# RWKV-7 recurrence and gated MoE on one core: the running product of w by a product tree over DRAM, in place of transposes, scan and transposes back

## The chip, the cores and the metric

One core of one Trainium2 chip. The time is device time in microseconds (us) of one execution, from the start of the program on the core to its end. The profile comes from one more execution, whose own time is given beside its span, the stretch from the first to the last instruction.

The engines are named as in the profile: PE is TensorE (PEld its weight loads), DVE is VectorE, ACT is ScalarE, POOL is GpSimd, SP is SyncE, which here does nothing but issue DMAs.

## The reference

B, H, S, D = 4, 8, 768, 40: four batches, eight heads, 768 tokens, 40 elements of a head. All inputs are float32.

```python
state = zeros(B, H, D, D)
for t in range(S):
    y[t]  = einsum('bhd,bhde->bhe', r[t], state)
    Sa    = einsum('bhde,bhe->bhd', state, a[t])
    state = state * w[t][:, :, None, :] - einsum('bhd,bhe->bhde', Sa, b[t])
    state = state + einsum('bhd,bhe->bhde', v[t], k[t])
x = y as (B*S, H*D)                       # 3072 x 320
h = x @ w_in                              # 320 x 2048
out = (h * cos(h)) @ w_out                # 2048 x 320
```

Only `w` and `a` matter for what follows. `w` decays each column of the state, so inside a chunk of tokens everything can be written with the running product W(t) = w(0) w(1) ... w(t), taken elementwise within the chunk: `a~` is a(t) times W(t-1), and k and b are divided by W(t).

## The kernel before

**Chunks.** The 768 tokens are cut into 24 chunks of C = 32. A natural tile (`nat[n, c]`, n one of w, a, b, k, v, r) has 128 partitions, batch times token, and in each partition 8 heads of 40 elements, padded to 64 for w, a and b (`DP`). Each such tile is loaded by `load` (L146): four DMAs, one for each batch, of 40 KB each. From chunk 4 on the tiles of w, a and b are double buffers, so a load waits until every reader of the tile two chunks earlier is done.

**W of a chunk.** `p1_w` (L331) does two chunks at a time. `turned` (L298) puts w by four PE transposes into PSUM as `wT`: partitions are (one of two heads, d), and the free axis is (pair of heads, batch, token), so tokens now lie in a row. ACT copies the first token of each row into `w1` (L336), DVE sets those places of `wT` to zero (L337), and a DVE scan over 512 elements (L340) computes state = state * w + w1. That is the running product, restarted at each row, and it is written to `wb`. POOL takes the last token's product as `wc` (L342), by which the state is decayed at the end of a chunk.

**What needs W in which layout.** `p1_a(c)` (one chunk at a time) brings W back by four PE transposes of `wb` into PSUM, `wn` (L353), because b and k need it as natural tiles. POOL then writes 1.0 into each row's first place of `wb` (L357), by which the same tile read one place earlier (`wx`) is W(t-1). PE transposes a into `aps`; DVE takes the reciprocal `rw` of `wn` (L361) and multiplies `aps` by `wx` to `aT` (L363); POOL multiplies b by `rw` to `bn` (L366). From chunk 4 on `wn` and `aps` share one PSUM tile. `p1_b` transposes `bn` of two chunks and ACT copies it (`bT`, L375); `p1_n` multiplies `bT` and `aT` for every batch and head into `nps`, and ACT copies the result into `nt` (L393).

**The inverse.** The unit triangular systems of four chunks are solved at once on DVE by `inverse`: a stream transpose `u` (L406), 31 steps of two instructions (L414, L418) and a stream transpose back, `rt` (L422). It begins when `nt` of four chunks is there.

**The recurrence of a chunk.** `main(c)` has five parts, which follow each other strictly: `ch_t` transposes the state `qz` (`sT`, L504; ACT copies `s`, L508), `ch_q` multiplies it by r (`qps`), `ch_x` builds the right side (`x0ps`, from `aT`, `qz`, `ag` and `vvm`), `ch_s` multiplies by `rt` (`sps`), and `ch_z` updates state and output (`dps`; `qz` on DVE and POOL L602/L603; `yt` L609/L614, the last times `wx`). Zeros that start a PSUM group in `ch_z` come from a matmul on the zero tile `idle`. Beside them `p2` prepares k, v, r of the next chunk: `p2_v` (`vT`, `rT`), `p2_k` (`kT`), `p2_g` (`gram`, `ag` L487, `vvm` L492).

**To the MoE.** `tokens(c)` writes `yt` to DRAM as `xd` (two DMAs, L623), and one step later `back` reads it as `xT` (three DMAs, L633/L635). Two chunks make one group of 256 tokens. A group and a quarter of d_ff are worked in pieces: `first_a` and `first_b` (`ph`, through the helper L101), the cosine by turns (ACT L676, DVE L678, ACT L682 and L683), the product `gT` (DVE L686), and two `second` (`po`, also L101), each of which goes out to DRAM after the last quarter.

**Weights of the MoE.** They come as 8-byte words, which `rounded` (L192) turns into float32: `fetch` (SP), `taken` (DVE and ACT), `mantissa` (DVE and ACT), `product` (DVE L229, POOL L232). These steps are spread over the first three chunks of the main loop.

**Order.** Nothing is scheduled automatically: every engine executes its instructions in the order in which the program issues them, and waits at each until its inputs and its output buffer are free. For each chunk a list `segs` holds the parts in that order; `M` is the place of an MoE piece. `step` issues one part, then the work that `later(n, work)` put n steps off (mostly DMA issues), then a few steps of the inverse and of the weights (`fill`). SP's queue is therefore also in program order: a DMA that waits holds those behind it.

```python
elif c == 2:
    segs, fill = [t, v, q, k, M, x, M, g, M, s, M, z, M, M], (0, 2)
```

`busy` and `shifted(N_PAD[c])` issue small PE matmuls whose results nobody reads; `shifted` stands at the head of chunks 2 and 19. PSUM has three pools with two buffers each: `ps_a` (two banks, `at(...)`: `wT`, `wn`, `bT`, `nps`, `sT` and so on), `ps_h` (`ph`) and `ps_o` (`po`).

Of the kernel before, what the change touches and what calls it, by code (L numbers as in the profile page):

```python
# [20 lines left out]
def kernel(  # L21
# [124 lines left out]
    def load(c, names, via=nc.sync):  # L146
        for n in names:
            for i in range(B):
                via.dma_start(
                    nat[n, c][blk[i], :, :D],  # L150
                    src[n][i, :, c * C : (c + 1) * C, :].rearrange("h t d -> t h d"),
                )

    for c in range(2):
        load(c, "w")
        load(c, "a", nc.scalar)
    for n, c in (("b", 0), ("b", 1), ("w", 2), ("w", 3), ("b", 2), ("b", 3)):
        load(c, n)
    load(0, "kvr")

# [14 lines left out]
    w1 = kept("w1", [P, 4 * B, C], 2, 0.0, on=nc.vector)  # L175
# [9 lines left out]
    idle = const.tile([P, 512], BF16, tag="idle", name="idle")  # L185
# [144 lines left out]
    def p1_w(c):  # L330
        ps = at("wT")  # L331
        for i in range(2):
            turned(ps[:, i], nat["w", c + i])

        for i in range(2):
            nc.scalar.copy(w1[i][:, :, 0:1], b4(ps[:, i])[:, :, 0:1])  # L336
        nc.vector.memset(ps[:, :, ::C], 0.0)  # L337
        for i in range(2):
            wb = ring.tile([P, 4 * P + 1], F32, tag="wb", name="wb")
            nc.vector.tensor_tensor_scan(wb[:, 1:], ps[:, i], flat(w1[i]), 0.0, ALU.mult, ALU.add)  # L340
            wc = ring.tile([P, 4 * B], F32, tag="wc", name="wc")
            nc.gpsimd.tensor_copy(wc, wb[:, C::C])  # L342
            G["wb", c + i], G["wc", c + i] = wb, wc

    def p1_a(c):
        if c < 4:
            wn = ps_h.tile([P, 512], F32, tag="h", name="wn")
            aps = ps_o.tile([P, 512], F32, tag="o", name="aps")
        else:
            ps = at("wn")  # L350
            wn, aps = ps[:, 0], ps[:, 1]
        for j in range(4):
            nc.tensor.transpose(  # L353
                wn[:, j * P : (j + 1) * P], G["wb", c][:, j * P + 1 : (j + 1) * P + 1], ident
            )

        nc.gpsimd.memset(G["wb", c][:, : 4 * P : C], 1.0)  # L357
        G["wx", c] = b4(G["wb", c][:, : 4 * P])
        turned(aps, nat["a", c])
        rw = ring.tile([P, H, D], F32, tag="rw", name="rw")  # L360
        nc.vector.reciprocal(rw, unpad(wn.rearrange("p (h d) -> p h d", h=H)))  # L361
        aT = ring.tile([P, 4, P], F32, tag="aT", name="aT")
        nc.vector.tensor_tensor(  # L363
            aT.rearrange("p j (b t) -> p (j b) t", b=B), b4(aps), G["wx", c], ALU.mult
        )
        nc.gpsimd.tensor_tensor(unpad(bn_b[c % 7]), unpad(nat["b", c]), rw, ALU.mult)  # L366
        G["rw", c], G["aT", c] = rw, aT
# [207 lines left out]
    def ch_z(c):  # L575
# [3 lines left out]
        for bb in range(B):  # L579
            for e in range(2):  # L580
                mm(
                    ps[bb // 2][full[e], bb % 2, : 4 * N72], idle[blk[bb], :DP],
                    idle[blk[bb], : 4 * N72], True,
                )
# [147 lines left out]
    def p1(c):  # L732


        def first_w():
            p1_w(c)
            if c == 4:
                for i in range(2):
                    later(1, lambda i=i: load(6 + i, "w"))

        def an_a(i):
            p1_a(c + i)
            if c == 4:
                later(1, lambda: load(6 + i, "ab"))
            elif i and c >= 2 and c + 3 < NCH:
                for m in range(6):
                    later(
                        9 + m // 3 if c == 2 else 2 + m, lambda m=m: load(c + 2 + m % 2, "wab"[m // 2])
                    )

        return [first_w, lambda: an_a(0), lambda: an_a(1), lambda: p1_b(c), lambda: p1_n(c)]
# [17 lines left out]
    with tc.manual_schedule():  # L769
# [24 lines left out]
        def busy(n, after=False):  # L794


            ps = ps_h.tile([P, 512], F32, tag="h", name="busy")
            if after:
                nc.vector.memset(tick, 1.0)
                nc.tensor.matmul(  # L800
                    ps[:1, :], lhsT=tick, rhs=idle, start=True, stop=True, skip_group_check=True
                )
            for _ in range(n):
                mm(ps, idle[:, :P], idle, True)
# [10 lines left out]
        for seg in (*first[:3], *other[:3], *first[3:], *other[3:]):  # L815
            step(seg)
# [5 lines left out]
        for n, seg in ((12, v), (0, k), (0, g), (6, main(0)[2]), (6, None), (4, v1), (0, k1), (0, g1)):  # L822
            for _ in range(n):
                inv_steps.pop(0)()
            if seg:
                step(seg)
            else:
                for m in range(3):
                    w_work[m][0]()
                p2_in(1)  # L830
                p2_kn(1)
        while inv_steps:
            inv_steps.pop(0)()
            if 2 < len(inv_steps) < 9:
                busy(1, True)
# [16 lines left out]
        N_PAD = {2: 56, 19: 48}  # L852
        M = object()
        for c in range(NCH):
# [8 lines left out]
            elif c == 2:  # L863
                segs, fill = [t, v, q, k, M, x, M, g, M, s, M, z, M, M], (0, 2)
            elif c == 3:
                pw4, pa4, pa5, pb4, pn4 = p1(4)
                pw, pa, pa1, pb, pn = p1(6)
                segs = [
                    t, pw4, M, q, pa4, M, x, pa5, M, s, pw, M, pb4, pa, M, pn4, pa1, M, z, M, pb, v,
                    pn, k, M, g,  # L870
                ]
                fill = (2, 3)
            elif c == 4:
                pw, pa, pa1, *p8 = p1(8)
                segs = [t, v, M, q, M, k, x, M, g, M, s, M, z, M, pw, M, pa, pa1, M]
                fill = (2, 0)
            elif c == 5:
                pw, pa, pa1 = p1(10)[:3]
                pb, pn = p8
                segs = [t, M, pb, q, M, pn, v, M, x, k, M, s, pw, M, g, M, z, M, pa, pa1, M]  # L880
            elif c % 4 == 0 and q0 < NCH:
                pb, pn = p1(q0)[3:]
                segs = [t, v, M, q, M, k, x, M, g, M, s, pb, M, z, M, pn, M, M]
            elif c % 4 == 1 and q0 < NCH:
                pw, pa, pa1 = p1(q0 + 2)[:3]
                segs = [t, M, pw, q, M, x, k, M, s, v, M, z, M, pa, M, g, M, pa1, M]
            elif c % 4 == 2 and q0 < NCH:
                pb, pn = p1(q0 + 2)[3:]
                segs = [t, M, pb, q, M, pn, v, M, x, M, s, k, M, g, M, z, M, M]
            elif c % 4 == 3 and q0 + 4 < NCH:  # L890
                fill = (2 if c == 7 else 1, 0)
                pw, pa, pa1 = p1(q0 + 4)[:3]
                segs = [t, M, pw, q, M, x, k, M, s, v, M, z, M, pa, M, g, M, pa1, M]
            else:
                segs = [t, v, M, q, M, x, k, M, g, M, s, M, M, z, M, M]
# [8 lines left out]
            if c in (2, 19):  # L904
                shifted(N_PAD[c])
# [58 lines left out]
```

## Time and profile before

| | |
|---|---|
| time, median of 3 runs | 847.02 us (846.65 to 847.22) |
| profiled execution: its own time | 844.89 us |
| profiled execution: span | 842.9 us, mean granted PE clock 0.952 |
| chain that ended last, by engine | PE 65%, DVE 23%, ACT 5%, issue 3%, DMA 2% |
| DMA | 49.10 MB, mean 58 GB/s |
| MoE matmuls `po`, `ph` (with its tail) | 226.4, 189.4 and 54.5 us of PE |
| inverse, L414 and L418 | 70.8 and 68.5 us of DVE |

The page is of one profiled execution. Part 1 gives each engine's busy time; part 2 cuts the span into 40 slices of 21 us and gives the busy share of each in tenths; part 4 follows the last instruction back to what released it; part 5 lists groups of instructions as "line engine operation output<-inputs shape xcount | busy, mean ns of one | idle time of the engine just before them, and what ended most of it". The timeline adds to each instruction its start in the span and its duration, and in square brackets a wait ahead of it with what ended it.

### The profile page before, as it was taken

The numbers are of one execution on the slowest core, as the hardware profiler recorded it, in microseconds if no ns is written. First come the engines' busy times: TensorE is split into PE (matmuls) and PEld (weight loads), VectorE is DVE, ScalarE is ACT, GpSimd is POOL, SyncE is SP. The second block draws the span as 40 slices with busy tenths as digits, with TensorE's granted clock in tenths as the row PEclk, the third lists the DMA queues.
The fourth block names the chain that finished last, engine by engine and source line by source line (L and its number), as shares of the span: only waits on it lengthen the run. The fifth ranks groups of instructions, "written<-read, shape, count | busy, mean of one in ns | idle before, by whom it ended". The sixth has DMA issues, their size and how long they took to land.

```text
span 842.9 us, 37607 instructions
## 1 busy us (share of the span) xinstructions
PE 750.5 (89%) x16830; PEld 575.3 (68%) x16830; DVE 511.0 (61%) x1076; ACT 377.1 (45%) x707; POOL 197.1 (23%) x343
## 2 busy tenths in 40 slices
PE   3547877995998979999998999998999999999997
PEld 3424556774676757778776777776777877777775
DVE  7688878778534696335797345796354774323331
ACT  1216676353153433545435436435445444454343
POOL 4405634230303203203221221230221222011000
PEclk9758698998898999999999999999999999999999
DMA  7456453431133212313224214214211212101000
GB/s 97 101 92 183 128 152 87 65 67 31 40 53 60 57 35 50 67 36 68 49 41 76 51 27 73 52 39 73 56 25 36 46 26 48 36 20 35 19 16 16
DMA packets 181856, 49.10 MB, mean 58 GB/s; under 512 B 156992, under 2 KB 178496, under 8 KB 181696
## 3 DMA queue, kind: packets, MB, share of 16 engines
q1 hardware_dynamic: 179264, 46.05, 26.6%
q8 instruction: 132, 2.16, 1.1%
q10 hardware_dynamic: 2176, 0.33, 0.3%
q0 software_dynamic: 256, 0.33, 0.2%
q14 instruction: 28, 0.23, 0.1%
HBM read 38.80 MB, written 7.86 MB: 55 GB/s over the span
## 4 chain that ended last, share of the span: by engine, by line
PE 65%; DVE 23%; ACT 5%; issue 3%; DMA 2%; SPq 1%; POOL 0%; ACTq 0%; DVEq 0%; POOLq 0%
PE ph L101 22%; PE po L101 19%; DVE inv_tmp L414 5%; DVE inv L418 5%; PE dps L101 3%; PE x0ps L101 3%; PE gram L101 2%; PE vT L298 2%; PE sps L101 2%; PE nps L101 2%; DVE turns L678 1%; DVE wb L340 1%; DVE rw L361 1%; PE qps L101 1%; PE bT L298 1%
## 5 line engine op out<-in xcount | busy, mean ns | idle before, releaser
L101 PE MATMUL po<-w_out_sb,gT 128*128 128x320 f32 x768 | 226.4, 442 | 0.0
L101 PE MATMUL ph<-xT,w_in_sb 128*128 128x256 f32 x768 | 189.4, 392 | 4.1 <-DVE gT L686 3.3
L101 PEld LDWEIGHTS po<-w_out_sb,gT 128*128 128x128 f32 x768 | 140.8, 191 | 54.1 <-issue 3.0
L101 PEld LDWEIGHTS ph<-xT,w_in_sb 128*128 128x128 f32 x768 | 143.1, 195 | 33.0 <-issue 12.9
L676 ACT ACTIVATE turns<-ph,rnd 128x512 f32<-128x512 f32 x96 | 63.8, 686 | 160.8 <-PE ph L101 160.2
L678 DVE SCALAR_TENSOR_TENSOR turns<-turns,ph 128x512 f32<-128x512 f32 x96 | 63.7, 684 | 110.0 <-ACT turns L676 109.8
L603 POOL TENSOR_TENSOR qz<-qz,wc 128x160 f32<-128x160 f32 x92 | 42.6, 482 | 254.5 <-DVE qz L602 254.0
L686 DVE TENSOR_TENSOR gT<-ph,turns 128x512 f32<-128x512 f32 x96 | 65.8, 686 | 36.8 <-ACT turns L683 36.8
L414 DVE TENSOR_TENSOR inv_tmp<-u,inv 128x31 f32<-128x31 f32 (+15 forms) x186 | 70.8, 381 | 4.5
L418 DVE TENSOR_TENSOR inv<-inv,inv_tmp 128x31 f32<-128x31 f32 (+15 forms) x186 | 68.5, 369 | 6.4
L683 ACT ACTIVATE turns<-turns,half_pi 128x512 f32<-128x512 f32 x96 | 69.3, 722 | 3.1
L682 ACT ACTIVATE turns<-turns 128x512 f32<-128x512 f32 x96 | 60.2, 627 | 21.5 <-DVE turns L678 21.5
L361 DVE RECIPROCAL rw<-wn 128x320 f32<-128x320 f32 x24 | 51.6, 2150 | 8.0 <-PE wn L298 7.7
L101 PE MATMUL ph<-xT,w_in_tail 64*128 64x256 f32 x384 | 54.5, 402 | 0.0
L602 DVE TENSOR_TENSOR qz<-dps,qz 128x160 f32<-128x160 f32 x92 | 28.9, 315 | 34.2 <-PE dps L101 34.1
L508 ACT COPY s<-sT 128x512 f32<-128x512 f32 x46 | 24.5, 585 | 51.9 <-PE sT L504 51.9
L101 PEld LDWEIGHTS ph<-xT,w_in_tail 64*128 64x128 f32 x384 | 33.0, 186 | 10.4 <-issue 6.8
L614 POOL TENSOR_TENSOR yt<-yt,wb 128x512 f32<-128x512 f32 x24 | 31.2, 1302 | 22.3 <-DVE yt L609 22.3
L436 POOL COPY vp<-nat_v 128x320 f32<-128x320 f32 x25 | 11.9, 475 | 99.4 <-DMA nat_v<-in_v_dram 69.3
L101 PE MATMUL sps<-x,rt 32*32 32x72 f32 x1536 | 22.3, 239 | 13.1 <-DVE rt L422 10.9
L101 PEld LDWEIGHTS sps<-x,rt 32*32 32x32 f32 x1536 | 17.8, 109 | 23.2 <-issue 16.5
L492 ACT COPY vvm<-gram 128x256 f32<-128x256 f32 x24 | 8.8, 367 | 51.7 <-DVE ag L487 51.4
(117 smaller groups left out, 1070.8 us busy)
## 6 DMA issues: line engine op xcount, KB each, us to landing
words<-in_moe_w_in_dram SPq DMA_DIRECT2D x8, 512.0 KB
nat_k<-in_k_dram SPq DMA_DIRECT2D x96, 40.0 KB
nat_v<-in_v_dram SPq DMA_DIRECT2D x96, 40.0 KB
nat_r<-in_r_dram SPq DMA_DIRECT2D x96, 40.0 KB
xd<-yt SPq DMA_DIRECT2D x48, 80.0 KB
out_dram<-ot SPq DMA_DIRECT2D x24, 160.0 KB
nat_w<-in_w_dram SPq DMA_DIRECT2D x88, 40.0 KB
nat_b<-in_b_dram SPq DMA_DIRECT2D x88, 40.0 KB
```

What stands on the lines that cost most here:

```text
L101: nc.tensor.matmul(o, lhsT=lhsT, rhs=rhs, start=start, stop=stop, skip_group_check=True)
L361: nc.vector.reciprocal(rw, unpad(wn.rearrange("p (h d) -> p h d", h=H)))
L414: nc.vector.tensor_tensor(tmp, u[:, j : j + 1, :j].to_broadcast([P, C - j, j]), x[:, j:, j : j + 1].to_broadcast([P, C - j, j]), ALU.mult,)
L418: nc.vector.tensor_tensor(x[:, j:, :j], x[:, j:, :j], tmp, ALU.subtract)
L602: nc.vector.tensor_tensor(z, pick(dp, 0, (2 * N72 + C, 2), (N72, 2), (1, D)), z, ALU.add)
L603: nc.gpsimd.tensor_tensor(z, z, wc.rearrange("p (f m b) -> p f m b", f=2, m=2)[:, :, :, bb] .unsqueeze(3).to_broadcast([P, 2, 2, D]), ALU. ...
L614: nc.gpsimd.tensor_tensor(yt.rearrange("p j b t -> p (j b) t"), yt.rearrange("p j b t -> p (j b) t"), wx, ALU.mult)
L676: nc.scalar.activation(n, u, ACTF.Identity, bias=rnd, scale=1.0)
L678: nc.vector.scalar_tensor_tensor(n, n, -ROUND, u, ALU.add, ALU.subtract)
L682: nc.scalar.activation(n, n, ACTF.Abs)
L683: nc.scalar.activation(n, n, ACTF.Sin, bias=half_pi, scale=-2.0 * math.pi)
L686: nc.vector.tensor_tensor(gT[:, 2 * e : 2 * e + 2].rearrange("p f t -> p (f t)"), us[e], ns[e], ALU.mult)
```

## The change

W is no longer scanned in the transposed layout. `w` of four chunks is fetched as one tile `ws` with (batch, head, chunk) in the 128 partitions and 32 tokens of 40 elements in each, 655 KB (`ws_fetch`). Nine DVE multiplications in place turn it into running products over the tokens, five up a tree and four down (`ws_scan`). The result is written to a DRAM tile `wd`, and the loads of w read from `wd` instead of from the input: `nat["w", c]` now holds W itself.

So `p1_w` has no scan: ACT copies the transposed W to `wb`, and POOL takes `wc` and writes the 1.0 there. The reciprocal (`over_w`) reads the natural tile directly, and the transposes back (`wn`) are gone with `w1` and its resets. `p1_a` handles both chunks of a pair in one part (one PSUM tile `aps` from chunk 4 on), with the second chunk's reciprocal after both `aT`; before chunk 4 each chunk's reciprocal stands ahead of its `aT`. `over_w` of a pair's first chunk stands in `p1_w` from chunk 4 on.

The trees stand on DVE: the first at the start; the second in chunk 2 as a part of its own after `ch_t`; the third in chunk 3 after `ch_x`; the fourth late in chunk 4; the others late in chunks 8 and 12. The fetch for the next tree follows three steps after a tree. In chunk 2 the loads of w for chunks 4 and 5 follow one step after the tree; those of a and b for these chunks come as before, a step earlier in number.

The padding of chunk 2 (56 small matmuls) becomes 128 at the start, ahead of the end of the first inverse; that of chunk 19 goes from 48 to 79. The tile `idle` is 128 wide instead of 512 and is read with a stride of 0 where 512 columns are wanted.

```diff
+                at_c = wd[c // 4][i, :, c % 4] if n == "w" else src[n][i, :, c * C : (c + 1) * C, :]
+                via.dma_start(nat[n, c][blk[i], :, :D], at_c.rearrange("h t d -> t h d"))
...
+    def ws_fetch(q, via=nc.sync):
+        n = 4 * C * D
+        via.dma_start(
+            ws.rearrange("p t d -> p (t d)"),
+            bass.AP(w.tensor, w.offset + q * n, [[S * D, B * H], [C * D, 4], [1, C * D]]),
+        )
+
+    def ws_scan(q, via=nc.sync):
+        n = 1
+        while n < C:
+            to = ws[:, 2 * n - 1 :: 2 * n]
+            nc.vector.tensor_tensor(to, to, ws[:, n - 1 :: 2 * n], ALU.mult)
+            n *= 2
+        n = C // 4
+        while n:
+            to = ws[:, 3 * n - 1 :: 2 * n]
+            nc.vector.tensor_tensor(to, to, ws[:, 2 * n - 1 : C - 1 : 2 * n], ALU.mult)
+            n //= 2
+        wd[q] = dram.tile([B, H, 4, C, D], F32, tag="wd", name="wd")
+        via.dma_start(wd[q].rearrange("b h c t d -> (b h c) (t d)"), ws.rearrange("p t d -> p (t d)"))
+
+    ws_fetch(0)
     for c in range(2):
+        load(c, "a", nc.scalar)
+    ws_scan(0, nc.scalar)
+    for c in range(2):
+        load(c, "b")
+    for c in range(4):
         load(c, "w")
-        load(c, "a", nc.scalar)
-    for n, c in (("b", 0), ("b", 1), ("w", 2), ("w", 3), ("b", 2), ("b", 3)):
-        load(c, n)
+    for c in range(2, 4):
+        load(c, "b")
     load(0, "kvr")
+    ws_fetch(1)
...
-        for i in range(2):
-            nc.scalar.copy(w1[i][:, :, 0:1], b4(ps[:, i])[:, :, 0:1])
-        nc.vector.memset(ps[:, :, ::C], 0.0)
         for i in range(2):
             wb = ring.tile([P, 4 * P + 1], F32, tag="wb", name="wb")
-            nc.vector.tensor_tensor_scan(wb[:, 1:], ps[:, i], flat(w1[i]), 0.0, ALU.mult, ALU.add)
+            nc.scalar.copy(wb[:, 1:], ps[:, i])
             wc = ring.tile([P, 4 * B], F32, tag="wc", name="wc")
             nc.gpsimd.tensor_copy(wc, wb[:, C::C])
+            nc.gpsimd.memset(wb[:, : 4 * P : C], 1.0)
+            G["wx", c + i], G["wc", c + i] = b4(wb[:, : 4 * P]), wc
+        if c >= 4:
+            over_w(c)
+
+    def over_w(c):
+        rw = ring.tile([P, H, D], F32, tag="rw", name="rw")
+        nc.vector.reciprocal(rw, unpad(nat["w", c]))
+        nc.gpsimd.tensor_tensor(unpad(bn_b[c % 7]), unpad(nat["b", c]), rw, ALU.mult)
+        G["rw", c] = rw

     def p1_a(c):
-        for j in range(4):
-            nc.tensor.transpose(
-                wn[:, j * P : (j + 1) * P], G["wb", c][:, j * P + 1 : (j + 1) * P + 1], ident
-            )
...
+        if c >= 4:
+            ps = at("aps")
+        for i in range(2):
+            if c < 4:
+                aps = (ps_h, ps_o)[i].tile([P, 512], F32, tag="ho"[i], name="aps")
+            else:
+                aps = ps[:, i]
+            turned(aps, nat["a", c + i])
+            if c < 4:
+                over_w(c + i)
+            aT = ring.tile([P, 4, P], F32, tag="aT", name="aT")
+            nc.vector.tensor_tensor(
+                aT.rearrange("p j (b t) -> p (j b) t", b=B), b4(aps), G["wx", c + i], ALU.mult
+            )
+            G["aT", c + i] = aT
+        if c >= 4:
+            over_w(c + 1)
...
+    def scanned(q):
+        ws_scan(q)
+        if q == 1:
+            for i in range(2):
+                later(1, lambda i=i: load(4 + i, "w"))
+        if q + 1 < NCH // 4:
+            later(3, lambda: ws_fetch(q + 1))
...
-                segs, fill = [t, v, q, k, M, x, M, g, M, s, M, z, M, M], (0, 2)
+                segs, fill = [t, lambda: scanned(1), v, q, k, M, x, M, g, M, s, M, z, M, M], (0, 2)
...
                 segs = [
-                    t, pw4, M, q, pa4, M, x, pa5, M, s, pw, M, pb4, pa, M, pn4, pa1, M, z, M, pb, v,
-                    pn, k, M, g,
+                    t, pw4, M, q, pa4, M, x, lambda: scanned(2), M, s, pw, M, pb4, pa, M, pn4, M, z, M,
+                    pb, v, pn, k, M, g,
                 ]
...
-                segs = [t, v, M, q, M, k, x, M, g, M, s, M, z, M, pw, M, pa, pa1, M]
+                segs = [t, v, M, q, M, k, x, M, g, M, s, M, z, M, pw, M, pa, lambda: scanned(3), M]
...
-                segs = [t, M, pw, q, M, x, k, M, s, v, M, z, M, pa, M, g, M, pa1, M]
+                segs = [t, M, pw, q, M, x, k, M, s, v, M, z, M, pa, M, g, M, M]
...
-        N_PAD = {2: 56, 19: 48}
+        N_PAD = {0: 128, 19: 79}
+        shifted(N_PAD[0])
```

## The prediction, made before the changed kernel ran

> **What bounds the kernel now.** First the page's busy shares and slices: they say which stage has which limit.
>
> ```profile
> PE 750.5 (89%) x16830; PEld 575.3 (68%) x16830; DVE 511.0 (61%) x1076; ACT 377.1 (45%) x707; POOL 197.1 (23%) x343
> PE   3547877995998979999998999998999999999997
> DVE  7688878778534696335797345796354774323331
> PEclk9758698998898999999999999999999999999999
> ```
>
> A slice is 21 us. From slice 16 TensorE (PE) is full, so work taken from it there is time. In the first seven VectorE (DVE) is full and PE is not; there a chain sets the time. Then the waits of PE (columns: total, times, longest) and the group rows name what the change touches:
>
> ```profile
> PE sps L101 <- DVE rt L422: 10.9, 2, 9.2
> PE wn L353 <- DVE wb L340: 8.3, 3, 3.9
> PE vT L298 <- DVE aT L363: 8.0, 3, 3.8
> L340 DVE TENSOR_TENSOR_SCAN wb<-wT,w 128x512 f32<-128x512 f32 x24 | 28.1, 1212 | 0.4
> L361 DVE RECIPROCAL rw<-wn 128x320 f32<-128x320 f32 x24 | 51.6, 2150 | 8.0 <-PE wn L298 7.7
> ```
>
> Scan and reciprocal cost DVE 80 us, and PE waits for their results some 16 us. Last, the timeline where the new transfers will stand:
>
> ```profile
> 31.73 1.25 DVE L406 STREAM_TRANSPOSE u<-nt 128x1024 f32<-128x1024 f32 x1 [5.11 <-ACT nt L393]
> ...
> 101.24 1.75 DVE L229 TENSOR_TENSOR w_out_sb<-mant,expo 128x512 f32<-128x512 f32 x1
> 102.47 0.72 SPq L623 DMA_DIRECT2D xd<-yt  x2
> 105.83 0.93 DVE L229 TENSOR_TENSOR w_in_sb<-mant,expo 128x512 f32<-128x512 f32 x1
> 105.90 0.38 SPq L633 DMA_DIRECT2D xT<-xd  x1
> 109.67 1.89 PE L101 MATMUL ph<-xT,w_in_sb 128*128 128x256 f32 x8
> ...
> 453.83 0.63 PE L298 MATMUL vT<-ident,vp 128*128 128x128 f32 x4 [3.77 <-DVE aT L363]
> ```
>
> The first inverse starts at 31.73; the first MoE matmul starts at 109.67, 2 us after SyncE's queue issued xT.
>
> [...]31, 256 and 512 elements take 0.19, 0.42 and 0.69 us, that is 0.16 us + 1.04 ns an element. [...]L229 took 1.75 us beside GpSimd work, 0.69 alone. [...]xT took 2.0 us (chain, 260.26 to 262.26); the busiest 4 us of this execution (40 to 44, by stretches) moved 324 GB/s. [...]after PE's 9.24 us wait the clock reads 0.50 from 208 to 216, and eight po take 4.63 us instead of 2.3.
>
> **The parts.** A product tree over four chunks is nine multiplies on 640, 320, 160, 80, 40, 40, 120, 280 and 600 elements: 9 x 0.16 + 2280 x 1.04 ns = 3.8, with 25 ns between dependent ones **4.0 us**. Six trees (24 us) replace 24 scans (28.1) and their resets (1.0), so DVE gains little in sum; the place matters.
>
> *Start.* Now w goes from DRAM to the transposes. In the changed program it is fetched as 128 rows (655 KB, issued 0.81; landing about 6.0 beside a and b, as the first two w chunks needed until 5.5 and 9.5), multiplied (4.0, with seven memsets of 0.21 in between: end 11.5), written (issue 0.45, [...]655 KB at 324 GB/s 2.0: lands 16.0) and read back by 16 DMAs on SP at 0.49 each (eight took 3.9): chunk 1 is issued by 20 and lands at 22. Then, with cold transposes (0.87 for four), copies of 0.59 and 2.15 + 0.63 for reciprocal and aT: wT 23.1, wb 24.2, aT(0) 24.8, rw(1) 27.0, bn(1) 27.9, bT 28.8 and copies 29.9, nps 30.8, aps(2, 3) 32.5, with aT(2) in that at 32.3, rw(3) 34.5, bn(3) 35.4, bT 36.3, copies 37.3, nps 38.2, nt 39.3. The inverse starts at 39.3 instead of 31.7: **+7.6** (6.0 to 9.5). The 128 pads (24.6 ns each by the 56 that took 1.5 us at 100 us) are 3 to 6 us in a PE wait of over 6 us for DVE: 0.
>
> *Chunk 2.* The second tree stands on DVE behind the L229 of 105.83, so at 106.76. GpSimd's L232 holds it 1.3 us: end 112.1. On SP the write of wd stands ahead of xd and waits for the tree; behind xd stand two weight loads, then eight loads of w(4), w(5), which wait for the write, then xT. So: write issued 112.5, landed 116.8; eight loads 3.9: 120.7; xT issued 121.0, landed 123.0 to 124.4 when the write moves at half that rate. PE was ready at 108.2 (the 56 pads gone): it waits about 15 us[...]. Against 109.67: 14.7 + 1.7 = **+16.4** (12 to 19.5). Removing the pads saves nothing here. Nothing behind absorbs it: x0ps, the x copy and the recurrence stand behind that ph on PE. The eight w loads of 40.95 (6.2 us of SP) go, but there SP is not late.
>
> *Chunk 3.* PE's 3.9 us wait for the scan and its half clock go: aps needs only a. ACT's qz now waits for a mant behind rw(4): x0ps about 145.6 instead of 149.9, -4.3. But nat_w(7) now waits for rw(5) on DVE, 16 loads and another write stand behind it on SP, so xT of chunk 3 comes at 180.3 where PE would want it at 178.5; 1.5 of that reaches the inverse. **-2.8** (0 to -4.5). The 9.2 us wait for rt stays: u and rt move together.
>
> *Chunks 4 to 23* (20 chunks). Four wn transposes are 0.44 us of full PE a chunk. Chunk 4: two chunks' 0.88, the wait for aT at sT 1.8, and wn behind the scan 0.7; the third tree costs 0.7 back at turns: **-2.7**. Chunk 5: 0, its pieces end in the chain xd, xT, ph (254 to 262). Chunk 7: DVE is full (9.4 to 9.6 of 10 us), so its two scans and reset, 2.4, count; plus 0.88 and a 0.4 wait of vT: **-3.7** (-1.5 to -5). Chunks 9, 13, 17: 3 x 0.88 = **-2.6**. Chunks 11, 15: vT waits 3.77 each because the second wn tile is held until the second reciprocal and aT; now both aT come first. 2 x (3.77 + 0.88) = **-9.3**, and the half clock after the one at 575 **-1.4** (0.79 in 574 to 582). The wb copies (24 x 0.59 - 3.1 = 11 us) lie on ACT at 45%: 0. Trees 4, 5 lie in DVE at 40 to 75%: **+0.5** (0 to 3). The trees' writes block SP until they are done, but xd and xT of those chunks stand ahead of them, and k, v, r behind are needed a chunk later. Pads at chunk 19: 79 for 48, 31 x 24.6 ns: **+0.8**.
>
> *Costed at nothing.* Fetches and writes add 12 x 655 KB = 7.9 MB to 49.1, where the 16 DMA engines are 10 to 40% busy; only their place in the queue counts. The reciprocal reads SBUF instead of PSUM; no row shows that. The nearest pair does: the 256-element product takes 0.42 us from SBUF (inv_tmp) and from PSUM (ag). So I take 2.15 and allow 0.1 either way, 2.4 us over 24 at most, most of it beside a full PE. GpSimd keeps its operations: wc and the reset of wb to one move from behind scan and wn to behind the copy, earlier; bn follows rw as before. The narrow zero tile is read with stride 0 for the same columns, so PE does the same.
>
> Sum: 7.6 + 16.4 - 2.8 - 2.7 - 3.7 - 2.6 - 9.3 - 1.4 + 0.5 + 0.8 = **+2.8 us**. The profiled execution is 844.9 us (span 842.9 and 2.0 around it), so 847.7 there; the median of the runs is 847.0, so **849.8**.
>
> **Rivals.** *B, faster: the xT wait is short.* It decides at chunk 2: if that costs under about 12 us, that is if ph starts before 120, the rest gains. With no sharing (tree ends 110.7), the write at the page's rate (111.1 + 3.5 = 114.6) and loads at the shortest SP issue seen (0.31, 2.5 us), xT lands at 119.4: cost 11.4; with a start of +6.0 the sum is -3.8: 843. For it: issues of 0.31 exist; against: eight w loads in a row took 3.9 to 6.2 in every place. *C, slower: SP becomes the bound through chunk 4.* At 0.6 us an issue (eight a took 5.0) chunk 2 costs 19, and some 45 issues between rw(5) and xT of chunk 3 add 5, so chunk 3 gives +3 instead of -2.8: about 859. Against: the SP rows between 140 and 180 are nearer 0.49. *D: the change does not do what it says*, xT not behind the loads: the program order of SP shows it behind, so little is left.
>
> **Numbers.** A (the sum) 0.57, B 0.23, C 0.18, D 0.02. A measurement of this kernel can tell about 0.2%, 1.7 us, from no change. A's 2.8 with an error of some 4 gives slower 0.43, same 0.12, faster 0.02; B faster 0.21, same 0.02; C slower 0.18; D faster 0.01, slower 0.01. So faster 0.24, same 0.14, slower 0.62. A's own range is 844 to 855; taking in B and most of C: 840 to 860. Signs are mixed, because +24 and -22 nearly cancel and each is known to a few us.
>
> **What would show it.** u (the first stream transpose) at 37 to 41; the first ph at 120 to 129 with a wait of 10 us or more on DMA xT, and SP's nat_w loads just ahead; nine ws multiplies adding to 4 us; no PE waits on wb, and none of vT on aT at chunks 11 and 15; from the first sps of chunk 4 to the end about 18 us less. It is wrong if the first ph follows the tree within 8 us, if a tree takes over 6 us, or if the late stage gains under 12.

## The result, and the profile after

The changed kernel takes **874.89 us** (median of 4 runs, 874.65 to 875.50) against 846.84 (846.19 to 847.22): a ratio of 1.0333, 95% interval 1.0315 to 1.0351. It is 28 us slower. Forecast were 849.8 us, and 840 to 860 as the range.

The page of the profiled execution of the changed kernel (span 873.0 us, granted clock 0.930): busy time, two rows of slices, and the row of the reciprocal.

```profile
PE 755.9 (87%) x16840; PEld 576.6 (66%) x16840; DVE 506.2 (58%) x1092; ACT 384.6 (44%) x706; POOL 197.8 (23%) x343
...
PE   1547748788689897999998999989999999999997
...
DVE  4688856776863479455389454697444775323322
...
PEclk9757768899898998999999999999999999999999
...
L377 DVE RECIPROCAL rw<-nat_w 128x320 f32<-128x320 f32 x22 | 47.2, 2143 | 7.9 <-DMA nat_w<-wd 7.9
```

DVE is busy 5 us less than before, ACT 8 us more (11 were costed). PE lost the 16.3 us of transposes back and is still busy 5 us more, so its other work took longer. Beyond that the page says only that PE's gaps got larger (755.9 of 873.0, against 750.5 of 842.9). PE's waits of the changed kernel name them (total, times, longest):

```profile
PE wT L328 <- DMA nat_w<-wd: 18.7, 2, 18.4
PE aps L328 <- DVE aT L393: 16.0, 10, 3.5
PE sps L101 <- DVE rt L453: 10.0, 2, 8.5
PE ph L101 <- DMA xT<-xd: 9.3, 3, 4.1
PE kT L328 <- issue: 7.3, 2, 6.5
...
PE aps L328 <- ACT wb L366: 2.3, 1, 2.3
```

The waits of `wn` for `wb` (8.3 us) and of `vT` for `aT` (8.0) are gone. In their place stand two that the kernel before did not have and the prediction did not name: `aps` for `aT`, ten times, once for each pair of chunks from 4 on, and `aps` for ACT's copy `wb`, once.

To see where the 30 us of the two spans (873.0 - 842.9) lie, take the start of the first `sm` on DVE of a chunk (part `ch_s` of the recurrence; L568 before, L599 after) and subtract the two executions. The differences of these offsets are what each stage cost:

| stage, by the first `sm` of chunk | forecast | changed | with the transposes first (e1) |
|---|---|---|---|
| start to 1 | +7.6 | +5.9 | +6.5 |
| 1 to 2 | +16.4 | +14.3 | +13.2 |
| 2 to 4 | -2.8 | +6.1 | +7.4 |
| 4 to 6 | -2.7 | -0.1 | -1.9 |
| 6 to 18 | -16.5 | -0.3 | -13.5 |
| 18 to the end | +0.8 | +4.3 | +3.1 |
| sum | +2.8 | +30.2 | +14.7 |

The two large losses, start and chunk 2, came in about the size that was forecast. **The gains that should have paid for them did not come**: 16 us in the late chunks and 9 in chunks 2 to 4.

The timeline of PE in the changed kernel at one of the ten waits (start, duration, in brackets the wait):

```profile
403.27 1.99 PE L101 MATMUL ph<-xT,w_in_sb 128*128 128x256 f32 x8
405.11 0.60 PE L328 MATMUL aps<-ident,nat_a 128*128 128x128 f32 x4
406.56 0.66 PE L328 MATMUL aps<-ident,nat_a 128*128 128x128 f32 x4 [0.85 <-DVE aT L393]
407.05 1.89 PE L101 MATMUL ph<-xT,w_in_sb 128*128 128x256 f32 x8
```

The four transposes of the first chunk end, PE stops until `aT` of that chunk has been computed on DVE, then come the four of the second chunk. Behind them wait MoE matmuls that need neither. Here DVE takes `aT` at once and 0.85 us is lost; at 469 and 591, where DVE is late, 3.5 us.

Chunk 2 in the changed kernel, all engines, shortened:

```profile
117.58 0.33 SPq L177 DMA_DIRECT2D wd<-ws  x1
118.01 1.00 SPq L654 DMA_DIRECT2D xd<-yt  x2
118.25 0.72 ACT L256 ACTIVATE mant<-mant,by_in 128x512 f32<-128x512 f32 x1 [4.86 <-DVE mant L253]
...
119.35 0.58 ACT L492 COPY rT<-vT 128x512 f32<-128x512 f32 x1
...
120.03 1.09 PE L328 MATMUL kT<-ident,kn 128*128 128x128 f32 x4 [6.49 <-issue]
...
120.74 3.83 SPq L151 DMA_DIRECT2D nat_w<-wd  x8
...
124.61 0.46 SPq L664 DMA_DIRECT2D xT<-xd  x1
...
126.92 1.62 PE L101 MATMUL ph<-xT,w_in_sb 128*128 128x256 f32 x3 [4.09 <-DMA xT<-xd]
```

Read it on SP: the write of `wd` waits until the tree on DVE is done (the tree runs from 112.79 to 117.55), `xd` stands behind it, then the eight loads of w, then `xT`; the first `ph` comes at 126.92 instead of 109.67. The tree holds PE in a second way: ACT stood 4.86 us at `mant`, which waits behind the tree, so the copies of `vT` and `rT` came late, and `kT` starts as soon as they end.

### The profile page after: what moved, and what is told of

Read it like the earlier page. It is cut to its first block, busy times and chain, and to the rows that moved or that the text cites. A ratio compares the mean times of both kernels' runs of the same rounds, so it can differ in the third digit from the quotient of the medians.

```text
span 873.0 us, 37674 instructions
## 1 busy us (share of the span) xinstructions
PE 755.9 (87%) x16840; PEld 576.6 (66%) x16840; DVE 506.2 (58%) x1092; ACT 384.6 (44%) x706; POOL 197.8 (23%) x343
## 3 DMA queue, kind: packets, MB, share of 16 engines
q8 instruction: 132, 2.16, 1.0%
## 4 chain that ended last, share of the span: by engine, by line
PE 63%; DVE 18%; ACT 5%; DMA 4%; issue 4%; SPq 3%; POOL 2%; DVEq 0%; ACTq 0%; POOLq 0%
PE ph L101 23%; PE po L101 20%; DVE inv_tmp L445 4%; DVE inv L449 4%; PE x0ps L101 3%; PE dps L101 3%; PE gram L101 3%; SPq L151 2%; PE vT L328 2%; PE sps L101 2%; DVE rw L377 2%; PE qps L101 1%; PE sT L535 1%; DMA nat_a<-in_a_dram 1%; PE nps L101 1%
## 5 line engine op out<-in xcount | busy, mean ns | idle before, releaser
L101 PE MATMUL ph<-xT,w_in_sb 128*128 128x256 f32 x768 | 194.0, 399 | 13.0 <-DMA xT<-xd 9.3
L101 PEld LDWEIGHTS po<-w_out_sb,gT 128*128 128x128 f32 x768 | 143.2, 194 | 56.4 <-issue 5.2
L101 PEld LDWEIGHTS ph<-xT,w_in_sb 128*128 128x128 f32 x768 | 146.1, 199 | 44.1 <-issue 18.6
L449 DVE TENSOR_TENSOR inv<-inv,inv_tmp 128x31 f32<-128x31 f32 (+15 forms) x186 | 71.4, 384 | 6.4
L377 DVE RECIPROCAL rw<-nat_w 128x320 f32<-128x320 f32 x22 | 47.2, 2143 | 7.9 <-DMA nat_w<-wd 7.9
L328 PE MATMUL aps<-ident,nat_a 128*128 128x128 f32 x88 | 16.3, 319 | 19.3 <-DVE aT L393 16.0
```

Of the source, the lines that this page charges most:

```text
L101: nc.tensor.matmul(o, lhsT=lhsT, rhs=rhs, start=start, stop=stop, skip_group_check=True)
L328: nc.tensor.transpose(ps[:, i * P : (i + 1) * P], x[:, 2 * i : 2 * i + 2].rearrange("p e d -> p (e d)"), ident)
L377: nc.vector.reciprocal(rw, unpad(nat["w", c]))
L449: nc.vector.tensor_tensor(x[:, j:, :j], x[:, j:, :j], tmp, ALU.subtract)
```

## The experiments

Each was timed in five rounds beside the kernel before on the same chip, whose medians were 846.7 to 847.5 us in the three groups of runs and in the last run. The changed kernel was timed apart from them, with 846.84 for the kernel before. What a run gained "over the changed kernel" is therefore a difference of medians of two groups; where the traces show the stage, that is the better evidence.

**Transposes first (e1).** From chunk 4 on all eight transposes of a pair stand ahead of the first `aT`.

```diff
-            turned(aps, nat["a", c + i])
             if c < 4:
+                turned(aps, nat["a", c + i])
                 over_w(c + i)
+            elif i == 0:
+                turned(ps[:, 0], nat["a", c])
+                turned(ps[:, 1], nat["a", c + 1])
```

> The changed kernel, but from chunk 4 on p1_a puts all eight transposes of a (both chunks of the pair) on PE before the first aT. Theory S (shared tile: the second chunk's four transposes wait for the first chunk's aT, which reads the same PSUM tile): ten waits of 16.0 us in total on PE and 1.7 us of half clock behind the one of 3.5 us vanish, so about 858 to 862 us instead of 874.9, and no PE wait of aps on aT is left. Rival R (DVE is late with aT whatever PE does; the wait only moves to sT, vT or gram, which need the buffer or aT): 870 to 876, with as many us of waits on aT under another name.

859.57 us, ratio to before 1.016 (1.0136 to 1.0183): 15.3 us less than the changed kernel. Its waits of PE begin

```profile
PE wT L328 <- DMA nat_w<-wd: 18.8, 2, 18.4
PE ph L101 <- DMA xT<-xd: 15.0, 3, 7.1
PE sps L101 <- DVE rt L456: 9.9, 2, 8.4
```

and PE's waits of `aps` for `aT` are gone; 2.3 us of `aps` for ACT's `wb` and 1.2 for a load of a are what the tile's view still shows. Chunks 6 to 18 now gain 13.5 us where 16.5 were forecast (table). But `ph` waits 15.0 us for `xT` instead of 9.3, and chunks 2 to 4 gain nothing: two of the waits of `aps` stood there, 3.9 us, and without them PE waits for the `xT` of 208 us for 7.1 us instead of 2.6.

**Two tiles (e11).** The order of the changed kernel, but a PSUM tile for each chunk.

```diff
-        if c >= 4:
-            ps = at("aps")
...
-                aps = ps[:, i]
+                aps = at("aps")[:, 0]
```

> The changed kernel, order unchanged, but from chunk 4 on each chunk's transposes of a go to a PSUM tile of their own instead of two halves of one. Theory S (it is the shared tile that makes the second chunk's transposes wait for the first chunk's aT): the ten waits of 16.0 us go, about 859 to 863 us; the pair now takes both buffers of the pool, so 1 to 3 us of waits for a buffer may come. Rival O (PE would wait for aT in this order whatever tile it writes): 872 to 876.

862.65 us, ratio 1.0179 (1.0157 to 1.02): 12.2 us less than the changed kernel, chunks 6 to 18 -12.0. With the order unchanged the waits of `aps` for `aT` fall from 16.0 us, ten times, to 0.2, once. So it is the shared tile and not the order by itself that makes PE wait: in the changed kernel the second half was not written before the first had been read. Theory S holds. The price of two buffers shows too: `aps` waits 1.7 us for ACT's `qz`, which holds a buffer, and `sT` and `gram` 1.5 us for `aT`, which e1 has not; e11 lies 3.1 us above e1.

**The padding at chunk 19 (e2).** `N_PAD` 48 instead of 79.

```diff
-        N_PAD = {0: 128, 19: 79}
+        N_PAD = {0: 128, 19: 48}
```

> The changed kernel with 48 small matmuls at chunk 19, as before, instead of 79. Theory P ([...]half clock for 3.4 us at 692 and a pause of 1.1 us in gram follow): 3 to 4 us less, 871 to 872. Rival (they cost only their own 31 x 24.6 ns, and the half clock has another cause): 0.8 us less, 874.

873.5 us, ratio 1.0308 (1.0284 to 1.0332). The gain of 1.4 us lies between the two expectations and within the spread of the runs. From the first `sm` of chunk 18 to that of 20 the offset to before rises by 1.1 us instead of 3.9, and the clock from 690 to 697, which the changed kernel has at 0.76, is 1.00. In this pair the half clock goes with the longer padding. The other traces make that weaker: of the six kernels here with 79, half clock begins right behind the padding in three (changed, e1, e12) and not in the other three (e3, e8, e11); of the eight with 48 it does so in none. So it came with 79 in half of the traces and with 48 in none; the length alone does not decide it.

**The second tree two parts later (e3).**

```diff
-                segs, fill = [t, lambda: scanned(1), v, q, k, M, x, M, g, M, s, M, z, M, M], (0, 2)
+                segs, fill = [t, v, q, lambda: scanned(1), k, M, x, M, g, M, s, M, z, M, M], (0, 2)
```

> The changed kernel with the second tree two parts later in chunk 2, behind ch_q, so that xd and xT of chunk 1 stand ahead of its write to DRAM and of the eight loads of w on SP. Theory Q (SP's queue holds xT): the first ph comes at about 114 to 117 us instead of 126.9, and 10 to 14 us are gained: 861 to 865. Rival D (tree and weights on DVE and ACT hold the first pieces, not the queue): ph is at most 4 us earlier, 870 or more.

869.52 us, ratio 1.0269 (1.0246 to 1.0292): 5.4 us gained. The first `ph` comes at 116.33, as theory Q expected, but the time does not follow. The timeline of e3:

```profile
120.93 0.33 SPq L177 DMA_DIRECT2D wd<-ws  x1
...
123.84 2.68 SPq L235 DMA_DIRECT2D words<-in_moe_w_out_dram  x3
...
129.12 0.43 DVE L243 TENSOR_SCALAR mant<-words 128x512 int32<-128x512 int32 x1 [3.60 <-DMA words<-in_moe_w_out_dram]
...
129.98 0.72 ACT L247 ACTIVATE expo<-expo,to_bits 128x512 int32<-128x512 int32 x1 [4.94 <-DVE expo L244]
...
131.15 1.25 ACT L707 ACTIVATE turns<-ph,rnd 128x512 f32<-128x512 f32 x2
...
136.03 0.77 PE L101 MATMUL ph<-xT,w_in_sb 128*128 128x256 f32 x1 [11.75 <-DVE gT L717]
```

The queue did hold `xT`, but that is not all that it holds. The write that waits for the tree now holds the words of `w_out`; DVE has none until 129.1, ACT waits 4.9 us at `expo`, the `turns` stand behind that, and PE waits 11.75 us for `gT`.

**e1, e2 and e3 together (e4).**

> All three edits together: eight transposes first, 48 at chunk 19, second tree behind ch_q. If the three causes are separate the gains add: 874.9 - 15 - 3 - 12 = 845, about the time of the kernel before (847). If they overlap (time saved in chunk 2 is waited for again later), 850 to 860.

857.5 us, ratio 1.0121 (1.0101 to 1.0142): 17.4 us less than the changed kernel, where the three alone sum to 22.1. They overlap. Two waits of PE are left over:

```profile
PE ph L101 <- DVE gT L720: 10.9, 1, 10.9
PE ph L101 <- DMA xT<-xd: 10.9, 2, 7.0
```

**The write behind the words (e5).** e4 with the write of the second tree three steps behind its multiplications.

```diff
-        ws_scan(q)
+        ws_scan(q, put=q > 1)
+        if q <= 1:
+            later(3 if q == 1 else 1, lambda: ws_put(q))
         if q == 1:
             for i in range(2):
-                later(1, lambda i=i: load(4 + i, "w"))
+                later(4 + i, lambda i=i: load(4 + i, "w"))
         if q + 1 < NCH // 4:
-            later(3, lambda: ws_fetch(q + 1))
+            later(6 if q == 1 else 3, lambda: ws_fetch(q + 1))
```

> e4 with the second tree's write to DRAM three steps behind its multiplications, and the eight loads of w(4), w(5) behind that. Theory Q (SP's queue, held by the write that waits for the tree, was what cost in e4 as well: the words of w_out stood behind the write, DVE had no words until 129, ACT's turns stood behind DVE's expo, and PE waited 10.9 us for gT): that wait falls to about 3 us as in the kernel before, chunk 2 costs 3 to 5 us instead of 9.5 against the kernel before, and the time falls by 5 to 8 us, to 850 to 853. Rival D (DVE and ACT are full of weights and tree, the queue is only named): the wait stays above 8 us and the time at 856 or more.

852.62 us, ratio 1.007 (1.005 to 1.0089): 4.9 us gained, just short of the 5 to 8; the time lies in the range of theory Q. Chunk 2 costs 5.2 us (1 to 2 in the sense of the table) after 9.6 in e4. The wait for `gT` fell only to 7.8, where theory Q expected 3: the queue was some 3 us of that wait, and the rest has another cause.

**The queue in chunk 3 (e6).** In the changed kernel SP itself waited for DVE (total, times, longest):

```profile
SPq L177 <- DVE ws L174: 22.5, 4, 10.4
...
SPq L151 <- DVE rw L377: 10.4, 2, 5.6
```

The loads of w wait for the reciprocal that reads the tile last; both these waits stand ahead of `xT` of chunk 3. The four waits for the trees stand elsewhere: the 10.4 us in chunk 2, the other three behind 250 us; the write of the third tree, in chunk 3, waited for nothing. e6 is e5 with

```diff
-                later(1, lambda: load(7, "w"))
-                for i in range(2):
-                    later(1, lambda i=i: load(6 + i, "ab"))
+                later(1, lambda: load(6, "ab"))
+                later(1, lambda: load(7, "w"))
+                later(1, lambda: load(7, "ab"))
```

and the third tree's write one step later.

> e5, and in chunk 3 the load of w(7) (which waits for a reciprocal on DVE) behind the loads of a(6) and b(6), and the third tree's write one step later. Theory Q (the wait of 7 us for xT of chunk 3 comes from SP standing 9 us behind rw and 5 us behind the tree): xT of chunk 3 is issued 3 to 6 us earlier against the work around it and 2 to 5 us are gained over e5. Rival (the 9 us wait of sps for rt takes it all back, since the inverse sets chunk 4): within 1 us of e5.

848.45 us, ratio 1.0012 (0.9999 to 1.0025): 4.2 us gained. The wait for `xT` at chunk 4 falls from 6.4 to 3.5 us, chunks 2 to 4 cost 3.5 us instead of 6.0. Ahead of that `xT` SP waits for `rw` once for 5.6 us instead of twice for 9.0; it waits for no tree there in e5 either, so what the later write adds is not shown. With the order mended, the change as a whole is level with the kernel before, and still pays 5.9 us at the start.

**The old start (e8 on the changed kernel, e7 on e6).** The first four chunks by scan and transposes back, one chunk at a time, with w from the input; the tree from chunk 4 on.

```diff
+            if c < 4:
+                p1_a_scan(c)
+                p1_a_scan(c + 1)
+                return
...
-        for seg in (*first[:2], other[0], *first[2:], *other[1:]):
+        for seg in (*first[:2], *other[:2], *first[2:], *other[2:]):
```

> The changed kernel with only its first four chunks as in the kernel before (scan and transposes back, w from the input); all else, padding included, as changed. Theory: u at 31.7 to 32.5 and 5 to 6 us gained, 869 to 870, since nothing between u and the late first ph gives it back. Rival: the tree of chunk 2 and the queue behind it set the first ph whatever the start does: within 2 us of 875.

872.91 us, ratio 1.0316 (1.0285 to 1.0348). The first inverse starts at 33.54 instead of 36.96 and the first `ph` comes 3.0 us earlier, but 2.0 us are gained, at the edge of what the rival allows. The 31.7 to 32.5 was missed by a pause of PE: in the middle of the last `nps` ahead of the inverse it stands still for 2.08 us at 31.05, with no releaser, where the kernel before stops for 0.45 us at the same matmul. The next run has more of them.

> e6 with the first four chunks as in the kernel before (scan, transposes back, one chunk at a time, w from the input), the padding of chunk 2 and 19 as before and none at the start: the tree is used from chunk 4 on. Theory: the way over DRAM costs the start 5.2 us at the first inverse; u comes at 31.7 to 32.5 and the time is 5 to 6 us under e6, so 840 to 843, faster than the kernel before. Rival (the start is hidden by the weights of the first three chunks, as DVE is full there): u earlier, but the first ph no more than 2 us earlier than in e6, and the time within 2 us of e6.

857.12 us, ratio 1.0125 (1.0099 to 1.0152): 8.7 us **slower** than e6, a clear miss. Yet the early stages did what was expected: at the first `sm` of chunk 4 the offset to before is 8.8 us instead of 14.3. It is lost late, by pauses of PE for which the timeline of e7 has no releaser:

```profile
732.54 0.21 PE L101 MATMUL gram<-rT,vT 40*32 40x32 f32 x1
732.55 0.19 PE L101 MATMUL gram<-aT,kT 40*32 40x32 f32 x1
732.55 0.59 PE L101 MATMUL gram<-rT,vT 40*32 40x32 f32 x46
734.78 0.30 PE L101 MATMUL gram<-rT,vT 40*32 40x32 f32 x16 [1.63 <-issue]
735.00 1.13 PE L101 MATMUL ph<-xT,w_in_tail 64*128 64x256 f32 x8
```

In the middle of 64 equal matmuls, whose operands are there, PE stops for 1.63 us. The page of e7 has one queue that fits:

```profile
q8 instruction: 132, 2.16, 1.1%
```

132 packets of 2.16 MB in all are 16 KB each, and PE's 2 x 16753 loads and matmuls are 254 for each packet. In the trace one packet lands at 733.28, and PE goes on 1.49 us later. At five other pauses of over 1 us, which end at 183.14, 447.76, 682.17, 705.99 and 763.87, a packet landed 1.47, 1.40, 1.44, 1.35 and 1.43 us earlier: the same distance six times.

The place in PE's stream leaves little room for chance. If PE's instructions come in these packets, PE should stop only where a packet begins. Number all instructions that the trace has of PE in order of their start, from 0. The pause at 734.78 stands ahead of number 30658, which is 449 + 118 x 256 + 1 (256 is near the 254 of the page), and 119 packets have landed by then. Of e7's 15 pauses of 0.5 us or more without a releaser, 13 stand at 449 + 256k or one further, with k + 1 packets landed; they add up to 15.4 us. The other two (`kT` at 80.91, behind ACT's copies, and `aps` at 329.26) don't, so they are not of this kind. In the 14 traces of this document together 56 such pauses stand at these places, each ending 1.2 to 1.6 us behind the landing. The profile names no releaser for them; that PE waits there for its own instructions is the author's reading, and it rests on these counts and distances. The pause of e8 at 31.05 is the one at number 449.

**The same order, the place in the stream moved (e9).**

```diff
-        N_PAD = {2: 56, 19: 48}
+        N_PAD = {0: 134, 19: 48}
+        shifted(N_PAD[0])
```

> e7 with 134 small matmuls during the first inverse instead of 56 at chunk 2, nothing else. PE then has as many instructions in all as in the kernel before (16831 matmuls for 16830), so the last chunks, whose order is the same, stand at the same places in its instruction stream. Theory F (the four pauses without a releaser, 1.4 to 1.9 us each, that PE makes from 682 on in e7 are waits for its own instructions, which arrive 16 KB at a time, 256 instructions[...]): the pauses are gone as in the kernel before, the offset to it stays at about +2 us from chunk 16 to the end, 846 to 849 us. Rival (the loss of the last chunks belongs to e7's order of work): the pauses stay, 855 or more.

840.45 us, ratio 0.9918 (0.9894 to 0.9943): 16.7 us less than e7 from useless matmuls alone, where 8 to 11 were expected. The four pauses of e7 from 682 on are gone; one of 1.08 us in `gram` stays, at 672. The same place in e9:

```profile
720.15 0.22 PE L101 MATMUL gram<-aT,kT 40*32 40x32 f32 x3
720.22 0.80 PE L101 MATMUL gram<-rT,vT 40*32 40x32 f32 x63
720.94 1.13 PE L101 MATMUL ph<-xT,w_in_tail 64*128 64x256 f32 x8
```

Of the 17.6 us between the spans of e7 and e9, 9.0 lie behind the first `sm` of chunk 18, 6.3 between those of 6 and 18, where e7 has a pause of 2.1 us at 448 and shorter ones, and 2.3 ahead of that. From the first `sm` of chunk 6 on e7 has 12.1 us of pauses at the places named above and e9 1.1; and behind two of them, at 682 and 764, e7's clock is half for 3.41 us each, which costs an estimated 3.4 us (half of the two stretches) and does not occur in e9. That makes 14.4 of the 15.3 us.

**Is that what ailed the changed kernel? (e12)** A like edit on it: 118 for 128 at the start, so that PE has as many matmuls as before.

> The changed kernel with 118 small matmuls at the start instead of 128, nothing else, so that PE has 16830 matmuls in all as in the kernel before and the last chunks stand at the same places in its instruction stream. Theory S (the loss of the changed kernel is the waits on aT and SP's queue; PE's pauses for instructions are 1.9 us of it, 1.1 of them in gram at 707, with a half clock of 1.7 us at 692): 1 to 4 us less, 871 to 874. Rival F (as in e7 against e9, where the same edit was worth 17 us, most of the loss is the place in the instruction stream): 860 or less.

874.99 us, ratio 1.0323 (1.0293 to 1.0353): no difference. The pause in `gram` at 707 is gone, the half clock at 692 stays, and the waits stay as they were:

```profile
PE wT L328 <- DMA nat_w<-wd: 18.8, 2, 18.2
PE aps L328 <- DVE aT L393: 16.0, 10, 3.5
```

Pauses at the places named above add up to 5.2 us in the changed kernel, 4.8 in e12 and 1.3 in the kernel before. The place in the stream explains e7, and at most 4 of the 28 us.

**The tree given out in pieces (e10).** e9 with the nine multiplications of the second tree two at a time over five parts.

```diff
+            if c == 2:
+                for i, work in enumerate(ws_ops()):
+                    later(4 + i // 2, work)
+                later(9, lambda: ws_put(1))
+                for i in range(2):
+                    later(10 + i, lambda i=i: load(4 + i, "w"))
+                later(12, lambda: ws_fetch(2))
```

> e9 with the nine multiplications of the second tree given out two at a time over five parts of chunk 2 (k, first piece, x, second piece, g), the write and the loads of w(4), w(5) behind them, and 137 small matmuls for the three filler matmuls that go. Theory T (in chunk 2 what is left is the tree as one block of 4.7 us on DVE, which holds mant, then ACT, then kT and turns): PE's wait for gT falls from about 8 to 4 us or less and 3 to 4.5 us are gained over e9: 842 to 845, faster than the kernel before. Rival (DVE is full there, so the pieces delay the weights and gT by as much in sum): within 1.5 us of e9.

836.39 us, ratio 0.988 (0.9852 to 0.9907), the fastest kernel of all; but its interval overlaps e9's and its profiled span is 1.1 us longer (839.3 against 838.2), so that it beats e9 is not shown. The medians differ by 4.1 us, as theory T forecast, but not where it said: PE's wait for `gT` fell from 8.1 to 6.8 us only, and at the first `sm` of chunk 2 it is 0.9 us ahead of e9. That the pieces delay the weights and `gT` nearly as much as the block does is likely, not shown. Both e9 and e10 beat the kernel before, by 0.8% and 1.2%.

## Why the prediction was wrong, point by point

**Start (+7.6): right, 1.7 too high.** The inverse starts at 36.96, not 39.3. The detour over DRAM was quicker than costed: the tree ends at 9.87 instead of 11.5, the write lands 3.58 us after its issue (10.74 to 14.32) instead of 4.0, and PE transposes w of chunk 1 at 19.77, where it was to land at 22. Of the 4.0, half was an estimate for what a write takes besides its bytes, from the 2.0 us of one `xT`. The tree took 4.1 us there and 3.94 to 4.76 elsewhere, for an estimate of 4.0. The largest excess is where GpSimd works beside it: the 320 elements took 1.32 us in chunk 2 and 1.03 in chunk 4, with POOL busy for 0.97 and 0.68 of that, and 0.49 in chunks 3, 8 and 12, with POOL idle.

**Chunk 2 (+16.4): right in size, in mechanism only in part.** It measured +14.3, and the order on SP was read rightly: the write, the loads, then `xT`. But the prediction has PE wait some 15 us for `xT`. It waits 4.09, after 6.49 at `kT`, which the tree holds by way of ACT's `mant` and copies. That path was left out, so the near size is in part luck. The 1.7 us in it for a slower clock behind the wait was the author's estimate; measured, the clock reads 0.50 from 116 to 132 and 0.84 from 132 to 134, so some 6 us of it lie behind the first `ph`. Mending the order of SP brings the stage from 14.3 to 9.6 (e3) and 5.2 us (e5): some 9 us were the queue, which held the words of `w_out` as well. The rest hardly falls when the queue is clear: PE waits 7.8, 8.1 and 6.8 us for `gT` in e5, e9 and e10, against 3.3 before.

**Chunk 3 (-2.8) and chunks 4 and 5 (-2.7): wrong, +6.1 and -0.1.** Two steps failed. The first is "PE's 3.9 us wait for the scan and its half clock go: aps needs only a". In the changed kernel stands there:

```profile
163.68 1.12 PE L328 MATMUL aps<-ident,nat_a 128*128 128x128 f32 x4 [2.29 <-ACT wb L366]
...
166.71 1.11 PE L328 MATMUL aps<-ident,nat_a 128*128 128x128 f32 x4 [1.91 <-DVE aT L393]
```

That is 4.2 us of waits for 3.9, and half clock from 163.4 to 170.2. `aps` needs a buffer besides a, and each wait ends when a reader of PSUM is done. By the first `sm` of chunk 3 2.9 of the 6.1 us are lost, where 4.3 were to be gained; e1, which has only the first of the two waits, still loses 1.3 there.

The second is "xT of chunk 3 comes at 180.3 where PE would want it at 178.5; 1.5 of that reaches the inverse". In the kernel before it was issued at 177.11, in the changed one at 206.06, 29 us later, while the work of PE ahead of it (`sT` of chunk 4) had moved by 23. PE then waits 2.6 us for it, and 7.1 in e1. The loads of w behind `rw` had been seen, but SP stands 10.4 us at the two reciprocals, and the prediction gives 180.3 without a working for that. This is part of rival C's mechanism; its price for this stage, +3, was nearer (its terms add up to 858, not 859). e6 shows it: with the loads in another order 4.2 us are gained. In chunks 4 and 5 two waits of `aps` for `aT`, 1.7 us, took the gain; e1, without them, has -1.9.

**Chunks 7 to 17 (-16.5): wrong, -0.3. This is the error.** The step is "now both aT come first", which was counted as the end of `vT`'s wait. That wait did end. But with both chunks in one part the program issues transposes, `aT`, transposes, `aT` in this order on one PSUM tile, and the program order that was read for SP was not read for that tile: the second four transposes wait until the first `aT` has read (ten times, 0.85 to 3.48 us). Over four chunks (first `sT` of chunk 9 to that of 13) the trade is 4.33 us of `aps` waits for 3.77 of `vT` waits, with 1.75 us of transposes back saved and 1.4 us lost that these waits do not account for: 121.6 us before, 121.8 after. No rival covered this, but the prediction's own sign did: a late stage that gains under 12 us. e1 shows that the forecast gain was real: -13.5 of -16.5 came as soon as the order within the pair was right, and e11 brings -12.0 with two tiles.

**The padding at chunk 19 (+0.8): right for the padding, wrong for the stage, +4.3.** Its own 31 matmuls took 0.77 us, as costed, and where nothing else came, in e3 and e11, the stage with 79 costs 1.0. Added came half clock for 3.4 us (692.4 to 695.8; an estimated 1.7 us lost, half of the stretch) and, in the one profiled execution, the pause of 1.13 us in `gram`, which stands at one of the places named above (number 449 + 109 x 256). PE was not idle ahead of the half clock: from 688 to 692, with the 79 one-column matmuls from 689.56 to 691.68, it is busy for 4.00 of 4.00 us. In three of six traces the clock fell right behind 79 of them; why is not shown.

**Costed at nothing, and right:** the reciprocal from SBUF takes 2143 ns against 2150 from PSUM, the `dps` matmuls on the narrow zero tile take 305 ns as on the wide one (medians), and the extra DMA traffic, 57.0 MB for 49.1, shows in no wait of PE, DVE or ACT behind 292 us.

**Open:** the 2.3 us between e7 and e9 ahead of chunk 6; the 1.3 us that e1 still loses by chunk 3; and the last 3 to 5 us of the wait for `gT` in chunk 2.

## What to carry to other kernels

When two producers and two consumers are merged into one segment, write down for each buffer, not only for each queue, who must have read it before the next may write: here two halves of one tile were one buffer (16.0 us of waits, 0.2 with two tiles), and all writes ahead of the first read left no such wait and were worth 15 us. A DMA that waits for a compute engine should be issued when its data is ready, not where it is made: every transfer behind it inherits the wait (10.4 us on SP in chunk 2), and clearing the first victim only shows the next. And when an edit that ought to help is slower, look for pauses without a releaser before giving it up.

## What the runs showed of the hardware that was not expected

A queue that the page calls "instruction" moves packets of 16 KB during the run (q8: 132 packets, 2.16 MB, in the kernel before, the changed one and e7), and PE makes pauses of 0.5 to 2.6 us with no releaser that end 1.2 to 1.6 us behind the landing of such a packet: 13 of them and 15.4 us in all in e7. They stand 256 instructions or a multiple of that apart. In the kernel before and the changed one they lie inside runs of short matmuls (`nps`, `gram`, `sps`, `pad`, 0.16 to 0.24 us each). That PE waits there for its own instructions is the author's reading. The work that is hit changed with the number of instructions ahead (e7, e9); how long PE pauses differs from kernel to kernel (0.45 us in the kernel before and 2.08 in e8 at the same matmul, number 449, behind the same work). Moving the padding and making it 78 matmuls longer changed the time by 16.7 us (e7 to e9, 857.12 to 840.45), more than most edits here, while on the changed kernel ten fewer changed nothing (874.89 to 874.99). So a single timing of a variant of this kernel carries an uncertainty that repeats of it don't show.
